# Fewer, larger first loads and four side-by-side first groups in a fused SiLU feed-forward kernel

## The chip, the cores and the metric

The kernel runs on one core of a Trainium2 chip. The metric is device time in microseconds of one execution. Only executions in the fast state are compared, and in each job the kernel before ran on the same chip as the others.

## The reference

The reference is a two-layer feed-forward block with SiLU, and its gradients. All inputs are bfloat16: x and grad_out are 2048 x 640, w1 is 640 x 1536, w2 is 1536 x 640.

```python
h = x @ w1
out = silu(h) @ w2
# outputs: out, and the gradients of x, w1 and w2 for grad_out
```

That is six matrix products of the same size: h, out, and four in the backward pass.

## The kernel before

The kernel works on the 2048 rows in four chunks of 512. In the first chunk it does, on the tensor engine (PE): 26 warm-up matmuls on a constant; 20 transposes of x (four row tiles of 128, five column blocks of 128) through PSUM; then 12 "h groups" of five 128x512 matmuls each, one group per block of 128 hidden columns; then the 60 matmuls of the first w2 phase, and so on. Only the start matters: what is loaded first, in which pieces, and what the first h matmuls wait for.

```python
# loads, in order of issue; nc.sync and nc.scalar are two DMA queues
load_x_tile(nc.sync, 0)      # x_nat[:, st, :], 128 rows x 640, 160 KB
load_x_tile(nc.scalar, 1)
load_x_tile(nc.sync, 2)
load_x_tile(nc.scalar, 3)
for lo, hi in ((0, 2), (2, DT)):          # row blocks of 128; DT = 5; FH = 256
    nc.sync.dma_start(out=w1_nat[:, lo:hi, 0:FH], in_=w1_v[:, lo:hi, 0:FH])
load_w1(FH, FC)                           # columns 256 to 512, all rows
for fc in range(1, NFC):
    load_w1(fc * FC, (fc + 1) * FC)       # columns 512 to 1024, 1024 to 1536
...
for hf in range(2):                       # w2 in two column halves
    nc.sync.dma_start(out=w2_nat[:, :, hf * DH:(hf + 1) * DH], in_=w2_v[...])
...
def pe_x_tile(xT, st):                    # per row tile: 5 transposes, 2 copies out of PSUM
    for lo, hi, copy in ((0, DS, nc.vector.tensor_copy), (DS, DT, nc.scalar.copy)):
        tp = ps_h.tile([P, hi - lo, P], dt_in, name="tp", tag="hp")
        for dt_ in range(lo, hi):
            nc.tensor.transpose(tp[:, dt_ - lo, :], x_nat[:, st, dt_ * P:(dt_ + 1) * P], ident[:])
        copy(out=xT[:, lo:hi, st * P:(st + 1) * P], in_=tp[:])
...
def h_group(ft, xT, aT, ghT):
    hp = ps_h.tile([P, SC], FP32, name="hp")
    for dt_ in range(DT):                 # five row blocks of w1, one after another
        nc.tensor.matmul(hp[:], lhsT=w1_nat[:, dt_, ft * P:(ft + 1) * P], rhs=xT[:, dt_, :],
                         start=(dt_ == 0), stop=(dt_ == DT - 1))
    # ... Silu and Tanh on ScalarE, two VectorE operations
...
for ft in range(FT):                      # FT = 12, first chunk
    h_group(ft, xT, aT, ghT)
```

Of the kernel before, what the change touches and what calls it, by code (L numbers as in the profile page):

```python
# [10 lines left out]
FP32 = mybir.dt.float32  # L11
# [4 lines left out]
def kernel(  # L16
# [11 lines left out]
    nc = tc.nc  # L28
    P = 128
# [6 lines left out]
    S, D = x2.shape  # L36
    F = w1.shape[1]
    ST, DT, FT = S // P, D // P, F // P
    SC = 512
    NCH = S // SC  # L40
    STC = SC // P
    DH = D // 2
    FC = 512
    NFC = F // FC
    LAG = 2
    NWARM = 26
    NFILL = 4
    dt_in = x.dtype
# [4 lines left out]
    ps_h = ctx.enter_context(tc.tile_pool(name="ps_h", bufs=8, space=bass.MemoryType.PSUM))  # L53
# [8 lines left out]
    x_nat = natpool.tile([P, ST, D], dt_in, name="x_nat")  # L62

    w1_v = w1.rearrange("(dt p) f -> p dt f", p=P)
    w2_v = w2.rearrange("(ft p) d -> p ft d", p=P)
    x_v = x2.rearrange("(st p) d -> p st d", p=P)
# [17 lines left out]
    with ExitStack() as mctx:  # L84
# [7 lines left out]
        warm = nc.const_aps.tensor(1.0, (P, P), dt_in)  # L92
        warm_a = cpool.tile([P, 1], FP32, name="warm_a")
        wp = ps_h.tile([P, SC], FP32, name="wp", tag="hp")
        for i in range(NWARM):
            nc.tensor.matmul(wp[:, 0:P], lhsT=warm, rhs=warm, start=True, stop=True)

        ident = cpool.tile([P, P], dt_in, name="ident")
        make_identity(nc, ident[:])

        w1_nat = w1pool.tile([P, DT, F], dt_in, name="w1_nat", tag="w1a")
        w2T = wpool.tile([P, DT, F], dt_in, name="w2T")
        w2_nat = wpool.tile([P, FT, D], dt_in, name="w2_nat")
# [9 lines left out]
            nc.sync.dma_start_transpose(out=goT[:], in_=go2[c * SC:(c + 1) * SC, :])  # L113
            return goT

        FH = FC // 2
        xT_next = xpool.tile([P, DT, SC], dt_in, name="xT")

        def load_w1(lo, hi):
            nc.sync.dma_start(out=w1_nat[:, :, lo:hi], in_=w1_v[:, :, lo:hi])  # L120

        def load_x_tile(eng, st):
            eng.dma_start(out=x_nat[:, st, :], in_=x_v[:, st, :])  # L123

        load_x_tile(nc.sync, 0)
        load_x_tile(nc.scalar, 1)
        load_x_tile(nc.sync, 2)
        load_x_tile(nc.scalar, 3)
        for lo, hi in ((0, 2), (2, DT)):
            nc.sync.dma_start(out=w1_nat[:, lo:hi, 0:FH], in_=w1_v[:, lo:hi, 0:FH])  # L130
        load_w1(FH, FC)
        for fc in range(1, NFC):
            load_w1(fc * FC, (fc + 1) * FC)
        nc.scalar.activation(warm_a[:], warm[:, 0:1], ACT.Silu)
        for hf in range(2):
            nc.sync.dma_start(out=w2_nat[:, :, hf * DH:(hf + 1) * DH], in_=w2_v[:, :, hf * DH:(hf + 1) * DH])
        goT_next = load_goT(0)
        for fc in range(NFC):
            nc.sync.dma_start_transpose(out=w2T[:, :, fc * FC:(fc + 1) * FC], in_=w2[fc * FC:(fc + 1) * FC, :])
        nc.sync.dma_start_transpose(out=w1T[:], in_=w1[:, :])  # L140

        DS = 3

        def pe_x_tile(xT, st):
            for lo, hi, copy in ((0, DS, nc.vector.tensor_copy), (DS, DT, nc.scalar.copy)):
                tp = ps_h.tile([P, hi - lo, P], dt_in, name="tp", tag="hp")
                for dt_ in range(lo, hi):
                    nc.tensor.transpose(tp[:, dt_ - lo, :], x_nat[:, st, dt_ * P:(dt_ + 1) * P], ident[:])  # L148
                copy(out=xT[:, lo:hi, st * P:(st + 1) * P], in_=tp[:])  # L149

        for st in range(STC):
            pe_x_tile(xT_next, st)
        for i in range(NFILL):
            nc.tensor.matmul(
                wp[:, 0:P], lhsT=ident[:], rhs=x_nat[:, STC - 1, 0:P], start=True, stop=True
            )

        def h_group(ft, xT, aT, ghT):
            hp = ps_h.tile([P, SC], FP32, name="hp")
            for dt_ in range(DT):  # L160
                nc.tensor.matmul(  # L161
                    hp[:],
                    lhsT=w1_nat[:, dt_, ft * P:(ft + 1) * P],
                    rhs=xT[:, dt_, :],
                    start=(dt_ == 0),
                    stop=(dt_ == DT - 1),
                )
            nc.scalar.activation(aT[:, ft, :], hp[:], ACT.Silu)  # L168
            t = tpool.tile([P, SC], FP32, name="t")
            nc.scalar.activation(t[:], hp[:], ACT.Tanh, scale=0.5)  # L170
            v = tpool.tile([P, SC], dt_in, name="v")
            nc.vector.tensor_scalar(out=v[:], in0=t[:], scalar1=-0.5, scalar2=0.5, op0=ALU.mult, op1=ALU.add)  # L172
            nc.vector.scalar_tensor_tensor(  # L173
                out=ghT[:, ft, :], in0=aT[:, ft, :], scalar=1.0, in1=v[:], op0=ALU.subtract, op1=ALU.mult
            )

        def g_group(ft, goT, ghT):
            gp = ps_h.tile([P, SC], FP32, name="hp")
# [32 lines left out]
        for c in range(NCH):  # L211
            xT, goT = xT_next, goT_next
            aT = apool.tile([P, FT, SC], dt_in, name="aT")
            ghT = apool.tile([P, FT, SC], dt_in, name="ghT")

            if c + 1 < NCH:
                xT_next = load_xT(c + 1)
                goT_next = load_goT(c + 1)
            if c == 1:
                for j in range(0, ST, STC):  # L220
                    nc.sync.dma_start(out=go_nat[:, j:j + STC, :], in_=go_v[:, j:j + STC, :])
            if c == 2:
                for j in range(STC, ST, STC):
                    nc.sync.dma_start(out=x_nat[:, j:j + STC, :], in_=x_v[:, j:j + STC, :])

            if c == 0:
                for ft in range(FT):
                    h_group(ft, xT, aT, ghT)
                nc.sync.dma_start(
                    out=aT_scr[:, c * SC:(c + 1) * SC].rearrange("(ft p) s -> p ft s", p=P), in_=aT[:]  # L230
                )
                sd_phase(c, w2_nat, aT, oT_scr)
                for ft in range(FT):
                    g_group(ft, goT, ghT)
                nc.sync.dma_start(
                    out=ghT_scr[:, c * SC:(c + 1) * SC].rearrange("(ft p) s -> p ft s", p=P), in_=ghT[:]
                )
                sd_phase(c, w1T, ghT, gxT_scr)
                continue

            for i in range(FT + LAG):
                if i < FT:
                    h_group(i, xT, aT, ghT)
                if i >= LAG:
                    g_group(i - LAG, goT, ghT)

            store_rows(c - 1, opool)
            nc.sync.dma_start(
                out=aT_scr[:, c * SC:(c + 1) * SC].rearrange("(ft p) s -> p ft s", p=P), in_=aT[:]
            )  # L250
            nc.sync.dma_start(
                out=ghT_scr[:, c * SC:(c + 1) * SC].rearrange("(ft p) s -> p ft s", p=P), in_=ghT[:]
            )
            if c == NCH - 1:
                load_a_blk(0, w1pool, "w1a")

            sd_phase(c, w2_nat, aT, oT_scr)
            sd_phase(c, w1T, ghT, gxT_scr)

    with ExitStack() as fctx:  # L260
        ab2pool = fctx.enter_context(tc.tile_pool(name="ab2pool", bufs=NFC - 1))
        gbpool = fctx.enter_context(tc.tile_pool(name="gbpool", bufs=NFC))
        fpool = fctx.enter_context(tc.tile_pool(name="fpool", bufs=NFC))
        s1pool = fctx.enter_context(tc.tile_pool(name="s1pool", bufs=3))

        for fc in range(1, NFC):
            load_a_blk(fc, ab2pool)
# [7 lines left out]

        gw2_v = gw2.rearrange("(ft p) d -> p ft d", p=P)
        g2T_v = g2T_scr[:].rearrange("(dt p) f -> p dt f", p=P)
        FB = FC // P
        k = 0
        for fc in range(NFC):  # L280
            a_blk = a_blks[fc]
            g2T = fpool.tile([P, DT, FC], dt_in, name="g2T")
            for dt_ in range(DT):
                gp = ps_h.tile([P, FC], FP32, name="hp")
                for st in range(ST):
                    nc.tensor.matmul(  # L286
                        gp[:],
                        lhsT=go_nat[:, st, dt_ * P:(dt_ + 1) * P],
                        rhs=a_blk[:, st, :],
                        start=(st == 0),  # L290
                        stop=(st == ST - 1),
# [8 lines left out]
        def store_gw2(fc):  # L300
            g2 = fpool.tile([P, FB, D], dt_in, name="g2")
            nc.sync.dma_start_transpose(out=g2[:], in_=g2T_scr[:, fc * FC:(fc + 1) * FC])
            nc.sync.dma_start(out=gw2_v[:, fc * FB:(fc + 1) * FB, :], in_=g2[:])

        gw1_v = gw1.rearrange("(dt p) f -> p dt f", p=P)
        k = 0
        for fc in range(NFC):
            gh_blk = gh_blks[fc]
            for dt_ in range(DT):
                if dt_ == DT // 2:  # L310
                    store_gw2(fc)
                if fc == NFC - 1 and dt_ == DT - 1:
                    for k, (lo, hi) in enumerate(((0, FC - P), (FC - P, FC))):
                        gp = ps_h.tile([P, FC], FP32, name="hp")
                        for st in range(ST):
                            nc.tensor.matmul(  # L316
                                gp[:, lo:hi],
                                lhsT=x_nat[:, st, dt_ * P:(dt_ + 1) * P],
                                rhs=gh_blk[:, st, lo:hi],
                                start=(st == 0),  # L320
                                stop=(st == ST - 1),
# [4 lines left out]
                        else:  # L326
                            nc.vector.tensor_copy(out=g1[:, lo:hi], in_=gp[:, lo:hi])  # L327
                        nc.sync.dma_start(
                            out=gw1_v[:, dt_, fc * FC + lo:fc * FC + hi], in_=g1[:, lo:hi]
# [3 lines left out]
                for st in range(ST):  # L333
                    nc.tensor.matmul(  # L334
                        gp[:],
                        lhsT=x_nat[:, st, dt_ * P:(dt_ + 1) * P],
                        rhs=gh_blk[:, st, :],
                        start=(st == 0),
                        stop=(st == ST - 1),
# [38 lines left out]
```

## Time and profile before

The time before is 322.19 us, median of three runs (321.62 to 322.34). In the profile PE is the tensor engine, PEld its loads of weights, DVE VectorE, ACT ScalarE, and SPq and ACTq the queues that issue loads. These lines are from the page of the kernel before: the span, the busy time of the engines, the chain that ended last by engine and by line, and the group of the h matmuls (busy us, mean ns of one, idle time before it and what ended most of it). Line 161 is the h matmul, line 196 a later phase.

```profile
span 320.5 us, 3556 instructions
...
PE 314.0 (98%) x1477; PEld 145.9 (46%) x1506; DVE 101.8 (32%) x179; ACT 78.6 (25%) x142; POOL 0.7 (0%) x6
...
PE 97%; DMA 1%; issue 1%; ACT 0%; SPq 0%; DVE 0%; DVEq 0%
PE hp L196 32%; PE hp L180 16%; PE hp L286 16%; PE hp L161 16%; PE hp L334 15%; DMA x_nat<-in_x_dram 1%; PE hp L316 1%; ACT xT L149 0%; PE tp L148 0%; SPq L123 0%; DVE g_2366 L327 0%; DVEq L327 0%
...
L161 PE MATMUL hp<-xT,w_nat 128*128 128x512 bf16 x232 | 56.4, 379 | 0.6 <-ACT xT L149 0.2
...
```

PE is busy 98% of the span and is 97% of the chain. The next lines are the timeline of PE in the first 9 us: start, duration, engine, line, operation, count, and in brackets the idle time before and its releaser. Line 148 is the transposes, 154 four filler matmuls, 161 the h matmuls.

```profile
...
start us, us, engine line op out<-in xcount [idle before <-releaser]
...
3.62 0.74 PE L148 MATMUL tp<-ident,x_nat 128*128 128x128 bf16 x10
5.32 0.73 PE L148 MATMUL tp<-ident,x_nat 128*128 128x128 bf16 x10 [0.96 <-DMA x_nat<-in_x_dram]
5.88 0.39 PE L154 MATMUL wp<-x_nat,ident 128*128 128x128 bf16 x4
6.48 2.75 PE L161 MATMUL hp<-xT,w_nat 128*128 128x512 bf16 x11 [0.21 <-ACT xT L149]
```

The first ten transposes (tiles 0 and 1) run at 3.62 us, the second ten only at 5.32, after a wait for x. The first h matmul starts at 6.48. From there 60 h matmuls take until 19.43, where the next phase begins: 12.95 us, or 60 times 215.8 ns, with nothing lost.

```profile
...
19.43 2.75 PE L196 MATMUL hp<-aT,w_nat 128*128 128x512 bf16 x12
...
```

The chain, in order of time (start, duration, what), names the same wait:

```profile
...
1.19 4.09 DMA x_nat<-in_x_dram
6.91 10.74 PE hp L161 x49
...
```

The DMA view, restricted to the first 5 us, gives for each group of loads its queue, count, size and the median time from issue to landing:

```profile
...
x_nat<-in_x_dram ACTq DMA_DIRECT2D x2, 160.0 KB, 3.7
x_nat<-in_x_dram SPq DMA_DIRECT2D x2, 160.0 KB, 3.5
...
w_nat<-in_w_dram SPq DMA_DIRECT2D x1, 192.0 KB, 4.3
w_nat<-in_w_dram SPq DMA_DIRECT2D x1, 128.0 KB, 4.1
```

A load is spread over 16 partial completions, and a wait ends with the last of them (the third x tile was complete at 5.27 us, and its transposes began at 5.32). The trace's completion records show how far the last is from the middle one (us from the span's start):

```
kernel before            8th of 16   16th of 16
x tile 0, 1              3.22, 3.39  3.57, 3.74
x tile 2, 3              4.01, 4.33  5.27, 5.50
w1 rows 0-256, 128 KB    4.73        5.78
w1 rows 256-640, 192 KB  5.43        6.43
w1 columns 256-512       6.51        7.39
```

### The profile page before, as it was taken

The page shows a single profiled execution, that of the slowest core. Times are in us where ns is not written, and L with a number is a line of the kernel's source. Part 1 is how long each engine was busy: PE and PEld are TensorE (multiplying, and loading weights), DVE is VectorE, ACT ScalarE, POOL GpSimd, SP SyncE. Part 2 cuts the span into 40 slices and gives each one's busy share as a digit, 9 for nine tenths or more (in the row PEclk, how much of TensorE's full clock was granted, in tenths as well). Part 3 has the DMA queues.
Part 4 walks back from the last instruction along what each step waited for, and adds up shares of the span by engine and source line. Part 5 has one row for each costly group of instructions (what it writes and reads, how often), then busy time and mean ns, then how long its engine had stood idle before and what let it go on. Part 6 is the DMA issues. An engine that isn't in the chain of part 4 may idle for free.

```text
span 320.5 us, 3556 instructions
## 1 busy us (share of the span) xinstructions
PE 314.0 (98%) x1477; PEld 145.9 (46%) x1506; DVE 101.8 (32%) x179; ACT 78.6 (25%) x142; POOL 0.7 (0%) x6
## 2 busy tenths in 40 slices
PE   7999999999999999999999999999999999999996
PEld 5444444444444444444444444444444444444443
DVE  1871551477510087810147741000000100001001
ACT  3960001555201255411054520110100001001100
POOL 0000000000000000000000000000000000000000
PEclk9999999999999999999999999999999999999999
DMA  8999999999699884392445079819999999995011
GB/s 246 316 192 209 254 265 253 320 271 277 215 229 336 203 237 122 118 319 66 127 159 141 2 254 268 217 25 293 262 240 263 249 203 343 251 281 181 33 49 35
DMA packets 149264, 66.69 MB, mean 208 GB/s; under 512 B 112640, under 2 KB 149248, under 8 KB 149248
## 3 DMA queue, kind: packets, MB, share of 16 engines
q1 hardware_dynamic: 148960, 66.13, 80.8%
q10 hardware_dynamic: 288, 0.33, 0.3%
q8 instruction: 12, 0.20, 0.2%
q14 instruction: 4, 0.03, 0.0%
HBM read 9.18 MB, written 28.97 MB: 119 GB/s over the span
## 4 chain that ended last, share of the span: by engine, by line
PE 97%; DMA 1%; issue 1%; ACT 0%; SPq 0%; DVE 0%; DVEq 0%
PE hp L196 32%; PE hp L180 16%; PE hp L286 16%; PE hp L161 16%; PE hp L334 15%; DMA x_nat<-in_x_dram 1%; PE hp L316 1%; ACT xT L149 0%; PE tp L148 0%; SPq L123 0%; DVE g_2366 L327 0%; DVEq L327 0%
## 5 line engine op out<-in xcount | busy, mean ns | idle before, releaser
L161 PE MATMUL hp<-xT,w_nat 128*128 128x512 bf16 x232 | 56.4, 379 | 0.6 <-ACT xT L149 0.2
L180 PE MATMUL hp<-goT,w2T 128*128 128x512 bf16 x238 | 56.8, 379 | 0.1
L196 PE MATMUL hp<-aT,w_nat 128*128 128x512 bf16 x235 | 52.2, 379 | 0.3
L196 PE MATMUL hp<-ghT,w1T 128*128 128x512 bf16 x235 | 52.2, 379 | 0.3
L286 PE MATMUL hp<-a_blk,go_nat 128*128 128x512 bf16 x236 | 51.8, 379 | 0.2
L334 PE MATMUL hp<-gh_blk,x_nat 128*128 128x512 bf16 x219 | 48.2, 379 | 0.3
L204 ACT ACTIVATE oT<-hp 128x512 bf16<-128x512 f32 x24 | 14.3, 597 | 110.0 <-PE hp L196 110.0
L168 ACT ACTIVATE aT<-hp 128x512 bf16<-128x512 f32 x48 | 28.7, 597 | 31.7 <-PE hp L161 31.7
L196 PEld LDWEIGHTS <-w_nat 128*128 128x128 bf16 x240 | 23.5, 98 | 28.3
L180 PEld LDWEIGHTS <-w2T 128*128 128x128 bf16 x240 | 23.5, 98 | 28.3
L286 PEld LDWEIGHTS <-go_nat 128*128 128x128 bf16 x240 | 23.5, 98 | 28.3
L161 PEld LDWEIGHTS <-w_nat 128*128 128x128 bf16 x240 | 23.4, 98 | 28.4 <-issue 0.4
L196 PEld LDWEIGHTS <-w1T 128*128 128x128 bf16 x240 | 23.4, 98 | 28.4
L206 DVE CAST oT<-hp 128x512 bf16<-128x512 f32 x16 | 11.1, 692 | 78.0 <-PE hp L196 78.0
L187 DVE SCALAR_TENSOR_TENSOR ghT<-ghT,hp 128x512 bf16<-128x512 bf16 x48 | 32.5, 682 | 7.3 <-PE hp L180 7.3
L334 PEld LDWEIGHTS <-x_nat 128*128 128x128 bf16 x224 | 21.9, 98 | 26.4
L173 DVE SCALAR_TENSOR_TENSOR ghT<-aT,v 128x512 bf16<-128x512 bf16 x48 | 33.0, 688 | 0.6
L172 DVE TENSOR_SCALAR v<-t 128x512 bf16<-128x512 f32 x48 | 20.5, 427 | 29.2 <-ACT t L170 29.2
L170 ACT ACTIVATE t<-hp 128x512 f32<-128x512 f32 x48 | 28.4, 591 | 0.0
L296 DVE CAST g2T<-hp 128x512 bf16<-128x512 f32 x7 | 4.8, 692 | 46.1 <-PE hp L286 46.1
L294 ACT ACTIVATE g2T<-hp 128x512 bf16<-128x512 f32 x8 | 4.8, 598 | 47.0 <-PE hp L286 40.7
L343 ACT ACTIVATE g_2140<-hp 128x512 bf16<-128x512 f32 x1 | 0.6, 597 | 13.6 <-DMA out_dram<-g_2077 13.6
(33 smaller groups left out, 29.3 us busy)
## 6 DMA issues: line engine op xcount, KB each, us to landing
aT_scr<-aT SPq DMA_DIRECT2D x4, 1536.0 KB, 6.7
ghT_scr<-ghT SPq DMA_DIRECT2D x4, 1536.0 KB, 8.0
out_dram<-o_sb SPq DMA_DIRECT2D x8, 640.0 KB, 3.4
oT_scr<-oT SPq DMA_DIRECT2D x4, 640.0 KB, 3.9
go_nat<-in_grad_out_dram SPq DMA_DIRECT2D x4, 640.0 KB, 8.1
gxT_scr<-oT SPq DMA_DIRECT2D x4, 640.0 KB, 4.7
w_nat<-in_w_dram SPq DMA_DIRECT2D x2, 960.0 KB, 10.9
x_nat<-in_x_dram SPq DMA_DIRECT2D x3, 640.0 KB, 7.8
```

The source lines that it names most:

```text
L161: nc.tensor.matmul(hp[:], lhsT=w1_nat[:, dt_, ft * P:(ft + 1) * P], rhs=xT[:, dt_, :], start=(dt_ == 0), stop=(dt_ == DT - 1),)
L168: nc.scalar.activation(aT[:, ft, :], hp[:], ACT.Silu)
L170: nc.scalar.activation(t[:], hp[:], ACT.Tanh, scale=0.5)
L172: nc.vector.tensor_scalar(out=v[:], in0=t[:], scalar1=-0.5, scalar2=0.5, op0=ALU.mult, op1=ALU.add)
L173: nc.vector.scalar_tensor_tensor(out=ghT[:, ft, :], in0=aT[:, ft, :], scalar=1.0, in1=v[:], op0=ALU.subtract, op1=ALU.mult)
L180: nc.tensor.matmul(gp[:], lhsT=w2T[:, dt_, ft * P:(ft + 1) * P], rhs=goT[:, dt_, :], start=(dt_ == 0), stop=(dt_ == DT - 1),)
L187: nc.vector.scalar_tensor_tensor(out=ghT[:, ft, :], in0=ghT[:, ft, :], scalar=1.0, in1=gp[:], op0=ALU.add, op1=ALU.mult)
L196: nc.tensor.matmul(op_[:], lhsT=w_all[:, ft, dt_ * P:(dt_ + 1) * P], rhs=rhs_all[:, ft, :], start=(ft == 0), stop=(ft == FT - 1),)
L204: nc.scalar.activation(oT[:, dt_, :], op_[:], ACT.Copy)
L206: nc.vector.tensor_copy(out=oT[:, dt_, :], in_=op_[:])
L286: nc.tensor.matmul(gp[:], lhsT=go_nat[:, st, dt_ * P:(dt_ + 1) * P], rhs=a_blk[:, st, :], start=(st == 0), stop=(st == ST - 1),)
L334: nc.tensor.matmul(gp[:], lhsT=x_nat[:, st, dt_ * P:(dt_ + 1) * P], rhs=gh_blk[:, st, :], start=(st == 0), stop=(st == ST - 1),)
```

## The change

The intent is to start h earlier and not to stall after that. x comes in three loads (1, 1 and 2 tiles) instead of four. The first 512 columns of w1 come as two row pieces (256 rows, 256 KB; 384 rows, 384 KB) instead of three pieces of half width. x is transposed by pairs of tiles, one copy per column block. And the first four h groups run side by side over w1's first 256 rows: eight matmuls need the first piece only, and while they run the second can land. As a side effect each DMA packet of the early w1 pieces is 1024 bytes instead of 512. w2 comes in one load, and the Tanh half of the SiLU work lags by four groups. The four filler matmuls now read the constant and not x.

```diff
-        load_x_tile(nc.sync, 0)
-        load_x_tile(nc.scalar, 1)
-        load_x_tile(nc.sync, 2)
-        load_x_tile(nc.scalar, 3)
-        for lo, hi in ((0, 2), (2, DT)):
-            nc.sync.dma_start(out=w1_nat[:, lo:hi, 0:FH], in_=w1_v[:, lo:hi, 0:FH])
-        load_w1(FH, FC)
+        load_x_tiles(nc.sync, 0, 1)
+        load_x_tiles(nc.scalar, 1, 2)
+        load_x_tiles(nc.sync, 2, STC)
+        load_w1_rows(nc.sync, 0, KM)      # w1_nat[:, lo:hi, 0:FC]; KM = 2
+        load_w1_rows(nc.sync, KM, DT)
...
-        for hf in range(2):
-            nc.sync.dma_start(out=w2_nat[:, :, hf * DH:(hf + 1) * DH], in_=w2_v[...])
+        nc.sync.dma_start(out=w2_nat[:], in_=w2_v[:])
...
+        def pe_x_pair(xT, st):
+            for dt_ in range(DT):
+                tp = ps_h.tile([P, 2, P], dt_in, name="tp", tag="hp")
+                for q in range(2):
+                    nc.tensor.transpose(tp[:, q, :], x_nat[:, st + q, dt_ * P:(dt_ + 1) * P], ident[:])
+                copy = nc.scalar.copy if dt_ % 2 else nc.vector.tensor_copy
+                copy(out=xT[:, dt_, st * P:(st + 2) * P], in_=tp[:])
...
+        def h_first(xT, aT, ghT):
+            hps = []
+            for ft in range(FB):                       # FB = 4
+                hps.append(ps_h.tile([P, SC], FP32, name="hp"))
+            for dt_ in range(KM):
+                for ft in range(FB):
+                    h_mm(hps[ft], ft, xT, dt_, dt_ + 1)
+            for i in range(FT + LAG_G):                # LAG_G = 4
+                if i < FT:
+                    if i < FB:
+                        h_mm(hps[i], i, xT, KM, DT)
+                    else:
+                        hps.append(ps_h.tile([P, SC], FP32, name="hp"))
+                        h_mm(hps[i], i, xT, 0, DT)
+                    silu_a(i, hps[i], aT)
+                if i >= LAG_G:
+                    silu_grad(i - LAG_G, hps[i - LAG_G], aT, ghT)
...
-                for ft in range(FT):
-                    h_group(ft, xT, aT, ghT)
+                h_first(xT, aT, ghT)
```

More of the change, by code (lines that the diff above doesn't have):

```diff
@@ L41 @@
     STC = SC // P
-    DH = D // 2
     FC = 512
     NFC = F // FC
+    FB = FC // P
     LAG = 2
+    LAG_G = 4
+    KM = 2
     NWARM = 26
@@ L114, in load_goT @@
             return goT
-        FH = FC // 2
         xT_next = xpool.tile([P, DT, SC], dt_in, name="xT")
@@ L120, in load_w1, with load_x_tiles, load_w1_rows @@
             nc.sync.dma_start(out=w1_nat[:, :, lo:hi], in_=w1_v[:, :, lo:hi])
-        def load_x_tile(eng, st):
-            eng.dma_start(out=x_nat[:, st, :], in_=x_v[:, st, :])
-        load_x_tile(nc.sync, 0)
-        load_x_tile(nc.scalar, 1)
-        load_x_tile(nc.sync, 2)
-        load_x_tile(nc.scalar, 3)
-        for lo, hi in ((0, 2), (2, DT)):
-            nc.sync.dma_start(out=w1_nat[:, lo:hi, 0:FH], in_=w1_v[:, lo:hi, 0:FH])
-        load_w1(FH, FC)
+        def load_x_tiles(eng, lo, hi):
+            eng.dma_start(out=x_nat[:, lo:hi, :], in_=x_v[:, lo:hi, :])
+        def load_w1_rows(eng, lo, hi):
+            eng.dma_start(out=w1_nat[:, lo:hi, 0:FC], in_=w1_v[:, lo:hi, 0:FC])
+        load_x_tiles(nc.sync, 0, 1)
[3 more added lines that the diff above has]
+        load_w1_rows(nc.sync, KM, DT)
         for fc in range(1, NFC):
@@ L134 @@
         nc.scalar.activation(warm_a[:], warm[:, 0:1], ACT.Silu)
-        for hf in range(2):
-            nc.sync.dma_start(out=w2_nat[:, :, hf * DH:(hf + 1) * DH], in_=w2_v[:, :, hf * DH:(hf + 1) * DH])
+        nc.sync.dma_start(out=w2_nat[:], in_=w2_v[:])
         goT_next = load_goT(0)
@@ L140, with h_mm @@
         nc.sync.dma_start_transpose(out=w1T[:], in_=w1[:, :])
-        DS = 3
-        def pe_x_tile(xT, st):
-            for lo, hi, copy in ((0, DS, nc.vector.tensor_copy), (DS, DT, nc.scalar.copy)):
-                tp = ps_h.tile([P, hi - lo, P], dt_in, name="tp", tag="hp")
-                for dt_ in range(lo, hi):
-                    nc.tensor.transpose(tp[:, dt_ - lo, :], x_nat[:, st, dt_ * P:(dt_ + 1) * P], ident[:])
-                copy(out=xT[:, lo:hi, st * P:(st + 1) * P], in_=tp[:])
-        for st in range(STC):
-            pe_x_tile(xT_next, st)
-        for i in range(NFILL):
-            nc.tensor.matmul(
-                wp[:, 0:P], lhsT=ident[:], rhs=x_nat[:, STC - 1, 0:P], start=True, stop=True
-            )
-        def h_group(ft, xT, aT, ghT):
-            hp = ps_h.tile([P, SC], FP32, name="hp")
-            for dt_ in range(DT):
+        def pe_x_pair(xT, st):
[5 more added lines that the diff above has]
+                copy(out=xT[:, dt_, st * P:(st + 2) * P], in_=tp[:])
+        pe_x_pair(xT_next, 0)
+        for i in range(NFILL):
+            nc.tensor.matmul(wp[:, 0:P], lhsT=warm, rhs=warm, start=True, stop=True)
+        pe_x_pair(xT_next, 2)
+        def h_mm(hp, ft, xT, lo, hi):
+            for dt_ in range(lo, hi):
                 nc.tensor.matmul(
@@ L167, in h_group, with silu_a, silu_grad @@
                 )
+        def silu_a(ft, hp, aT):
             nc.scalar.activation(aT[:, ft, :], hp[:], ACT.Silu)
+        def silu_grad(ft, hp, aT, ghT):
             t = tpool.tile([P, SC], FP32, name="t")
@@ L175, in h_group @@
             )
+        def h_group(ft, xT, aT, ghT):
+            hp = ps_h.tile([P, SC], FP32, name="hp")
+            h_mm(hp, ft, xT, 0, DT)
+            silu_a(ft, hp, aT)
+            silu_grad(ft, hp, aT, ghT)
+        def h_first(xT, aT, ghT):
[15 more added lines that the diff above has]
+                    silu_grad(i - LAG_G, hps[i - LAG_G], aT, ghT)
         def g_group(ft, goT, ghT):
@@ L277 @@
         g2T_v = g2T_scr[:].rearrange("(dt p) f -> p dt f", p=P)
-        FB = FC // P
         k = 0
```

## The prediction

> **What bounds the kernel now.** The tensor engine: busy 98% of the 320.5 us span on the page, 97% of the chain of waits. The main work is 1440 matmuls of 128x512, 215.8 ns apart in the timeline. The Trainium skill, "TensorE: Matmul & The Clock Gate", section "Back-to-back issue gap", gives N/2.4+2.5 ns, 216 for 512, as the warm gap: the trace agrees. So 1440 x 0.2158 = 310.8 us is fixed. The first such matmul starts at 6.48 us; the last output follows the last matmul by 3 us. The 60 matmuls of the first h phase take 6.48 to 19.43, exactly 60 gaps: no stall after the start. The change can only move the start, unless it makes a new stall.
>
> **What sets 6.48.** The four x tiles (160 KB each, two per queue) land at 3.57, 3.74, 5.27 and 5.50 us (DMA landings). Most of a tile's 16 partial completions come about 1 us earlier (tile 3: eighth at 4.33, last at 5.50): one DMA engine lags, with three packets of about 400 ns instead of 55. The Trainium skill, "DMA: Bandwidth & Descriptors", section "Why a DMA increments its semaphore by 16 and not by 1", says only the full count means all landed; the trace shows the wait ending on the last. Then: transposes to 6.05, last DVE copy to 6.33, matmul at 6.48, 0.98 us after the last landing. The w1 pieces land at 5.78, 6.43 and 7.39, only just off the path.
>
> **What the change does.**
> - x: the same 640 KB, but on SP's queue tiles 2 and 3 go wholly before w1. In the kernel before, w1 had moved perhaps a third of its first 8 KB per engine before tile 3 was in, some 0.13 us. Last x landing about 5.35.
> - Transposes by pair: the first h matmul needs only the first column block (two transposes, one 128x256 copy, estimated 0.29 us from 358 ns for 384 columns). Landing to matmul about 0.8 us instead of 0.98.
> - w1's first piece grows from 128 to 256 KB. 1024-byte packets take 47 to 51 ns (27 for 512 bytes), so 16 per engine is about 0.8 us: landing about 6.1, a tie with the copy.
> - First h matmul about 6.15, gain 0.3 us.
> - The eight side-by-side matmuls buy 8 x 0.216 = 1.7 us, to about 7.9, before w1's second piece (about 7.2) is needed. No stall.
> - The lag of 4 delays tanh and DVE work by about 2.7 us; PSUM's eight buffers cover it. The backward groups need ghT 13 us later. Nothing on the path.
> - w2 in one load must be whole by about 19.1; both halves were in at 17.76 before, and larger packets are no slower.
>
> **Time.** 322.19 - 0.35 = 321.8 us; 8 in 10: 321.0 to 322.4. Faster by over 2%: 0.005; within 2%: 0.99; slower: 0.005.
>
> **What would show it.** First 128x512 matmul of h at 6.0 to 6.3 us, and 12.95 us from it to the next phase's first; its releaser w1's first piece or the second pair's first copy; last x landing 5.2 to 5.4; no PE idle at the ninth h matmul; everything after shifted by one constant.
>
> **What would make it wrong.** The lagging DMA engine may be an accident of a run: without it the start comes up to 1 us earlier (about 5.4); with a worse one the change shows nothing. A stall at the ninth matmul (second w1 piece late), at the first w2 matmul, or on PSUM would cost. The range of before's three runs, 0.7 us, is as large as the gain.

## The result and the profile after

The changed kernel took 322.19 us (median of four runs, 321.70 to 322.71), the kernel before 322.21 us (four runs, 321.62 to 322.34). The ratio of the fast runs is 1.0003 with a 95% interval of 0.998 to 1.0027: the same. A ratio here is the record's own comparison of the fast runs; it is close to the ratio of their means, and not quite that of the medians quoted beside it. A second sample of five runs, below, gave 1.0013 (1.0000 to 1.0026). There is no gain to be seen, and in these few runs the times of the changed kernel are more spread: over 1.0 and 1.2 us in the two samples, against 0.7 and 0.6 us for the runs of before beside them.

The lines of the page of the changed kernel that answer to those above; line 158 is now the h matmul:

```profile
span 320.0 us, 3585 instructions
...
PE 315.9 (99%) x1506; PEld 146.1 (46%) x1506; DVE 101.5 (32%) x181; ACT 77.5 (24%) x142; POOL 0.7 (0%) x6
...
PE 97%; DMA 2%; SPq 0%; issue 0%; DVE 0%; DVEq 0%
...
L158 PE MATMUL hp<-xT,w_nat 128*128 128x512 bf16 x240 | 57.0, 379 | 0.5 <-DVE xT L149 0.4
...
```

The profiled run was one of the changed kernel's faster ones (321.79 us). The timeline of PE from 3.5 us; line 147 is the transposes:

```profile
...
3.93 1.58 PE L147 MATMUL tp<-ident,x_nat 128*128 128x128 bf16 x20
5.88 1.90 PE L158 MATMUL hp<-xT,w_nat 128*128 128x512 bf16 x8 [0.37 <-DVE xT L149]
7.93 1.25 PE L158 MATMUL hp<-xT,w_nat 128*128 128x512 bf16 x5
```

h starts at 5.88 us, 0.60 us earlier than in the kernel before. But eight matmuls later the tensor engine has to wait: the ninth starts at 7.93. The weight loads (PEld) say for what:

```profile
...
5.88 1.41 PEld L158 LDWEIGHTS <-w_nat 128*128 128x128 bf16 x8 [0.54 <-DMA w_nat<-in_w_dram]
7.93 0.33 PEld L158 LDWEIGHTS <-w_nat 128*128 128x128 bf16 x3 [0.64 <-DMA w_nat<-in_w_dram]
```

Both starts wait for w1: the first piece, complete at 5.84, and the second, complete at 7.89. The line of PE above names a copy (`DVE xT`) for the first start instead, and the last copy on DVE did end at 5.84 too. But the first h matmul needs only column block 0 of both pairs, and by the instruction records the copy of that block, the fourth on DVE, ended at 5.40; in three_again h started at 6.06, before the last two DVE copies had ended (6.17 and 6.56). So w1's first piece cost about 0.44 us even in this trace. The copies:

```profile
...
4.31 1.53 DVE L149 COPY xT<-tp 128x256 bf16<-128x256 bf16 x6 [4.31 <-PE tp L147]
...
```

The chain has changed its first link from x to w1's second piece, issued at 2.16 us. It counts the phase after h (L221) from the end of the last h matmul, 19.33; the first matmul of that phase starts at 19.17:

```profile
...
2.16 5.72 DMA w_nat<-in_w_dram
7.93 11.40 PE hp L158 x52
19.33 12.95 PE hp L221 x60
...
```

```profile
...
19.17 3.19 PE L221 MATMUL hp<-aT,w_nat 128*128 128x512 bf16 x14
...
```

The loads of the first 5 us in the DMA view:

```profile
...
w_nat<-in_w_dram SPq DMA_DIRECT2D x1, 384.0 KB, 5.7
x_nat<-in_x_dram SPq DMA_DIRECT2D x1, 320.0 KB, 3.5
w_nat<-in_w_dram SPq DMA_DIRECT2D x1, 256.0 KB, 4.2
x_nat<-in_x_dram ACTq DMA_DIRECT2D x1, 160.0 KB, 3.2
x_nat<-in_x_dram SPq DMA_DIRECT2D x1, 160.0 KB, 3.0
...
```

The second piece took 5.7 us from issue to landing, at 7.89. The h phase is 13.28 us long instead of 12.95, so 0.33 of the 0.60 us are given back, and the next phase begins at 19.17 instead of 19.43, about 0.26 us earlier. From there to the last matmul it is 297.83 us in both traces (and in every fast trace), so nothing later in the kernel changes: the Tanh lag and the single w2 load cost nothing.

That makes one number useful for the rest: the **effective start**, the start of the phase after h minus 12.95 us, which is when h would have to start to reach that point without a stall. It is 6.48 us in the trace of before and 6.22 in this trace of after. A run's time minus its effective start is 315.6 to 315.9 us in all thirteen fast traces, so the time of a run is, to about 0.15 us, its effective start plus a constant.

### The profile page after: what moved, and what is told of

The parts are those of the page before. It is cut to its first block, busy times and chain, and to the rows that moved or that the text cites. A ratio compares the mean times of both kernels' runs of the same rounds, so it can differ in the third digit from the quotient of the medians.

```text
span 320.0 us, 3585 instructions
## 1 busy us (share of the span) xinstructions
PE 315.9 (99%) x1506; PEld 146.1 (46%) x1506; DVE 101.5 (32%) x181; ACT 77.5 (24%) x142; POOL 0.7 (0%) x6
## 4 chain that ended last, share of the span: by engine, by line
PE 97%; DMA 2%; SPq 0%; issue 0%; DVE 0%; DVEq 0%
PE hp L221 32%; PE hp L205 16%; PE hp L309 16%; PE hp L158 16%; PE hp L357 15%; DMA w_nat<-in_w_dram 2%; PE hp L339 1%; SPq L124 0%; SPq L127 0%; DVE g L350 0%; DVEq L350 0%
## 5 line engine op out<-in xcount | busy, mean ns | idle before, releaser
L221 PE MATMUL hp<-aT,w_nat 128*128 128x512 bf16 x240 | 52.5, 379 | 0.0
L221 PE MATMUL hp<-ghT,w1T 128*128 128x512 bf16 x240 | 52.5, 379 | 0.0
L167 ACT ACTIVATE aT<-hp 128x512 bf16<-128x512 f32 x48 | 30.0, 627 | 33.3 <-PE hp L158 33.3
L221 PEld LDWEIGHTS <-w_nat 128*128 128x128 bf16 x240 | 23.5, 98 | 28.3
L221 PEld LDWEIGHTS <-w1T 128*128 128x128 bf16 x240 | 23.4, 98 | 28.4
L171 ACT ACTIVATE t<-hp 128x512 f32<-128x512 f32 x48 | 29.9, 628 | 0.0
L368 DVE CAST g<-hp 128x512 bf16<-128x512 f32 x7 | 4.8, 692 | 47.0 <-PE hp L357 26.3
```

Of the source, the lines that this page charges most:

```text
L167: nc.scalar.activation(aT[:, ft, :], hp[:], ACT.Silu)
L171: nc.scalar.activation(t[:], hp[:], ACT.Tanh, scale=0.5)
L221: nc.tensor.matmul(op_[:], lhsT=w_all[:, ft, dt_ * P:(dt_ + 1) * P], rhs=rhs_all[:, ft, :], start=(ft == 0), stop=(ft == FT - 1),)
```

## The experiments

Twelve more runs were made; with the first two that is fourteen traces of ten kernels. This table has one row per fast trace, in us from the span's start, from the trace's completion and instruction records. The first w1 piece is given with its size and its 8th and 16th completion; "full clock" is where the granted clock of PE (the share of full speed that it is allowed) is first recorded as full (the first three-piece trace has no such record; there the transposes go from 107 ns apart to 56 ns at about 4.5 us).

```
trace            x last  first w1 piece        second  full clock  h first  h long  eff. start  run
before           5.50    128 KB  4.73 / 5.78   6.43    3.67        6.48     12.95   6.48        322.23
before_again     4.75    128 KB  4.93 / 5.11   6.18    6.57        6.35     13.04   6.44        322.20
x_only_again     4.57    128 KB  4.70 / 5.17   6.07    3.49        5.78     12.95   5.77        321.50
after            4.74    256 KB  5.20 / 5.84   7.89    4.06        5.88     13.28   6.22        321.79
after_again      4.54    256 KB  5.09 / 6.71   8.68    4.66        6.75     13.20   7.01        322.67
no_second_piece  4.60    256 KB  5.28 / 6.73   7.82    6.55        6.78     12.96   6.79        322.44
w2_halves        4.69    256 KB  5.06 / 6.96   8.01    4.33        7.00     12.96   7.02        322.78
in_order         4.63    256 KB  5.17 / 6.08   7.46    3.44        6.12     13.92   7.09        322.80
w1_first         5.74    256 KB  4.07 / 4.32   8.11    3.65        6.45     12.95   6.45        322.02
packets_512      4.85    128 KB  4.71 / 5.24   5.66    6.35        6.06     13.50   6.61        322.35
three_pieces     4.46    128 KB  4.80 / 5.88   6.55    -           5.92     12.96   5.94        321.57
three_again      4.72    128 KB  4.67 / 5.86   6.63    6.07        6.06     12.96   6.07        321.85
five_pieces      4.66    128 KB  4.77 / 5.57   5.97    6.72        6.06     13.61   6.72        322.58
```

Two things must be kept in mind when these rows are compared. The clock: in five traces it is late (6.07 to 6.72), and the transposes are then 107 ns apart instead of 56; with the changed loads they keep PE busy until 6.06, which is where h starts in three_again, packets_512 and five_pieces, so a first piece that lands before that cannot show there. The chip: before_again and experiments 2 to 4 ran on chip 13; x_only, packets_512, three_pieces and w1_first on 6; the other four on 12 (the chip of the first comparison is not on record). The three latest first pieces (6.71, 6.73, 6.96) are all of chip 13. On chip 12 alone, 256 KB landed at 6.08, 128 KB of the same packets at 5.86 and 5.57, and 128 KB of 512-byte packets at 5.17: the order is the same, the differences are smaller. How much of the late landing belongs to the chip was not tested.

### 1. The kernel before, again

No edit. The question was whether the slow x tiles of the first trace belong to the kernel.

> The kernel before, unchanged, for a second trace of its start. If one lagging DMA engine belongs to the kernel, the last x landing is again 5.3 to 5.6 us, about 1 us after the eighth of its sixteen completions, and h starts at 6.4 to 6.6 us. If the lag is an accident of the run, the last x landing moves by several tenths of a microsecond, and h's start with it. Time ratio to before 1.000 within 0.002.

Measured: 322.20 us (321.73 to 322.39), ratio 1.0002 (0.9989 to 1.0015). The last x tile landed at 4.75 us, not 5.50. So the late x on which my reading of the start rested does not belong to the kernel in every run. h nevertheless started at 6.35. The timeline of PE says why:

```profile
...
3.71 2.32 PE L148 MATMUL tp<-ident,x_nat 128*128 128x128 bf16 x20
...
6.35 2.84 PE L161 MATMUL hp<-xT,w_nat 128*128 128x512 bf16 x12
```

The 20 transposes took 2.32 us; in a trace where the clock was up early, ten of them take 0.73 (experiment 8). In this trace the full clock is recorded only from 6.57 us, so the transposes were slow and the first h matmuls too. Two different causes gave nearly the same effective start, 6.48 and 6.44. That is chance.

The Trainium skill, "TensorE: Matmul & The Clock Gate", section "What's actually happening", describes a clock gate that opens after a busy window of about 3.4 us, and says that the window is free-running and the opening therefore differs from run to run. The traces agree that it differs, but not in size: the page puts the variation at 500 ns either way, and here, with the same 26 warm-up matmuls from 0.78 us on, the full clock is recorded from 3.44 to 6.72 us. In four traces it is there by 3.67, less than 3 us after the first matmul, so a whole busy window was not needed. I had cited this page and left this part out of the prediction.

### 2. The changed kernel, again

No edit.

> The changed kernel, unchanged, for a second trace. Theory A (the late second w1 piece belongs to the change): h starts at about 5.9 us, the second piece lands again at 7.5 us or later, and the ninth h matmul waits 0.2 us or more. Rival B (the slow packets were an accident of that run): the second piece lands near 7.2 us or earlier and there is no wait. Time ratio to before 0.999 to 1.000.

Measured: 322.25 us (322.03 to 323.23), ratio 1.0013 (1.0000 to 1.0026). This is the weight-load timeline:

```profile
...
6.75 1.41 PEld L158 LDWEIGHTS <-w_nat 128*128 128x128 bf16 x8 [1.36 <-DMA w_nat<-in_w_dram]
8.72 0.33 PEld L158 LDWEIGHTS <-w_nat 128*128 128x128 bf16 x3 [0.56 <-DMA w_nat<-in_w_dram]
```

Theory A holds for the second piece, and a worse part, which I had not expected, comes on top: the first piece landed at 6.71, so h started at 6.75, 0.87 us later than in the other trace of the same kernel, although the eighth of its sixteen completions was in at 5.09. Then the ninth matmul waited again for the second piece, which landed at 8.68; this cost 0.25 us. The effective start is 7.01. The lag passes from load to load: the sixteenth completion trails the fifteenth by 0.84 us in the first piece, and by 1.19, 1.24 and 1.23 us in the three loads behind it.

### 3. Without the second piece (wrong result)

```diff
-                    lhsT=w1_nat[:, dt_, ft * P:(ft + 1) * P],
+                    lhsT=w1_nat[:, (dt_ % KM) if wrong else dt_, ft * P:(ft + 1) * P],
...
-                        h_mm(hps[i], i, xT, KM, DT)
+                        h_mm(hps[i], i, xT, KM, DT, wrong=True)
```

> Wrong h on purpose: the first four groups read w1's first piece again in place of the second, so nothing waits for the second. If the wait at the ninth matmul is what ate the rest of the gain, then h takes 12.95 us again from its first matmul to the next phase's first, which comes about 0.33 us earlier than in the changed kernel, 0.6 us earlier than before; time ratio to before about 0.998. If the wait was a symptom and the time is limited by something later (third w1 piece, ACT, PSUM), a wait of the same size appears later in the h phase.

Measured: 322.23 us (321.63 to 322.48), ratio 1.0002 (0.9988 to 1.0015); the output is wrong, as meant. h took 12.96 us: the wait is gone and no other appeared later, as the theory said. But the gain did not come: the expected ratio was about 0.998, the interval begins at 0.9988. In its trace the first piece landed at 6.73 and held h until 6.78. PE in this trace:

```profile
...
6.78 1.47 PE L158 MATMUL hp<-xT,w_nat 128*128 128x512 bf16 x6 [0.51 <-DMA w_nat<-in_w_dram]
```

So removing the second piece's wait is not enough for the gain; in this trace the first piece holds h. The wait may still have a price: beside the 1.0013 of the changed kernel in the same job, 1.0002 is about 0.3 us less, as much as the wait cost in the traces (0.33 and 0.25), but the intervals overlap.

### 4. w2 in two halves again

```diff
-        nc.sync.dma_start(out=w2_nat[:], in_=w2_v[:])
+        for hf in range(2):
+            nc.sync.dma_start(out=w2_nat[:, :, hf * DH:(hf + 1) * DH], in_=w2_v[:, :, hf * DH:(hf + 1) * DH])
```

> The changed kernel with w2 loaded in two halves as before. Rival C: the queue's free slot made the transposing load of grad_out be issued at 4.7 us instead of 9.9, and its preparation slowed the packets of w1's second piece. Then, with the issue late again, the second piece lands near 7.2 us and the ninth matmul does not wait. If C is wrong the second piece lands within the spread of the other traces of the changed kernel (about 7.9) and the wait stays.

Measured: 322.78 us (321.80 to 323.01), ratio 1.0016 (1.0003 to 1.0029), so a little slower than before. The first piece landed at 6.96 and the second at 8.01. With the later issue of grad_out's load restored, the pieces are as late as ever: rival C falls. There was no wait at the ninth matmul here only because h itself began at 7.00.

### 5. and 8. Only the x loads changed

```diff
-        load_x_tile(nc.sync, 2)
-        load_x_tile(nc.scalar, 3)
+        nc.sync.dma_start(out=x_nat[:, 2:STC, :], in_=x_v[:, 2:STC, :])
```

> The kernel before with only the x loads changed (tiles 2 and 3 in one load on SP's queue). Effective start is the first matmul of the phase after h minus 12.95 us; it was 6.47 and 6.44 in two traces of before and 6.22, 7.01 and 7.02 in three of the changed loads. Theory D (the larger w1 pieces with 1024-byte packets are what comes late): here w1's pieces stay as before, so the first lands at 5.1 to 5.9 and does not hold h; x lands at about 4.6, and effective start is 5.7 to 6.4, the lower end where the PE clock is up before the transposes. Time ratio to before 0.998 to 1.000. Rival E (moving x ahead only moves the slow packets onto w1): the first w1 piece lands at 6.2 or later here too, no gain.

Measured: 322.12 us as the median of the four fast runs (321.73 to 322.34), ratio 1.0005 (0.9992 to 1.0019). The fifth execution took 481.20 us, and it was the profiled one. Its span and granted clock:

```profile
...
core 0: 479.3 us, clock 0.658
...
```

That trace is not used for times. Its loads landed as elsewhere, x at 4.58 us and the first w1 piece at 4.96. The kernel ran again:

> The kernel before with only the x loads changed, again, because its profiled run fell in a state with a clock of 0.658. x lands at about 4.6, w1's first 128 KB piece in 512-byte packets at 5.0 to 5.8, and effective start is 5.7 to 6.6; which of the two decides depends on whether the PE clock is up before the transposes (start about 5.7) or after (about 6.3). Ratio to before 0.999 to 1.001: without the larger pieces there is neither the loss of the changed kernel nor a sure gain.

Measured: 322.01 us (321.50 to 322.23), ratio 0.9996 (0.9984 to 1.0008). In its trace the clock was up at 3.49 us:

```profile
...
3.55 0.73 PE L147 MATMUL tp<-ident,x_nat 128*128 128x128 bf16 x10
4.61 0.73 PE L147 MATMUL tp<-ident,x_nat 128*128 128x128 bf16 x10 [0.33 <-DMA x_nat<-in_x_dram]
...
5.77 3.40 PE L160 MATMUL hp<-xT,w_nat 128*128 128x512 bf16 x14 [0.21 <-ACT xT L148]
```

The last x landed at 4.57, the first w1 piece (128 KB) at 5.17, and h started at 5.78 without a stall. With the small pieces the first w1 piece does not hold h, as theory D expected; E, that x ahead makes w1 late, falls. But the mean time does not fall below that of before either (0.9996 and 1.0005, both intervals across 1): the one late x of the first trace is not what a typical run loses.

### 6. w1's row pieces as column halves

```diff
-        load_w1_rows(nc.sync, 0, KM)
-        load_w1_rows(nc.sync, KM, DT)
+        for lo, hi in ((0, KM), (KM, DT)):
+            for cl in (0, FC // 2):
+                nc.sync.dma_start(out=w1_nat[:, lo:hi, cl:cl + FC // 2], in_=w1_v[:, lo:hi, cl:cl + FC // 2])
```

> The changed kernel with each w1 row piece loaded as two column halves, so the packets are 512 bytes again and the volume before the first and the second piece is the same. If the slow packets come with the 1024-byte form, there are few here (under 12 over 150 ns between 3.5 and 6.5 us, against 18 to 27 in the changed kernel) and both halves of the first piece land by 5.9. If they come with the volume or the hour, the first piece lands at 6.2 to 7.0 again, and effective start stays near 7.0.

Measured: 322.35 us (321.68 to 322.49), ratio 1.0008 (0.9996 to 1.0021). The first 256 rows were in at 5.66 us (halves at 5.24 and 5.66), the rest at 7.00, and 11 packets between 3.5 and 6.5 us took over 150 ns (26 and 27 in the two traces of the changed kernel, 6 and 11 in those of before). So the expectation for the smaller form is met. Two things changed at once, though: packets of 512 bytes, and loads of half the size. And the time was not gained: the next load, columns 512 to 1024, was in only at 10.87, and the h phase was 13.50 us long (about 0.39 us of the excess is this wait, 0.15 the late clock).

### 7. w1's first columns in three pieces

```diff
-    KM = 2
+    KM = 3
...
-        load_w1_rows(nc.sync, 0, KM)
-        load_w1_rows(nc.sync, KM, DT)
+        for lo, hi in ((0, 1), (1, 3), (3, DT)):
+            load_w1_rows(nc.sync, lo, hi)
```

> The changed kernel with w1's first 512 columns in three pieces of 128, 256 and 256 rows, and the first three row blocks side by side. If volume per piece sets when h starts, the first piece (128 KB) lands at 5.0 to 5.9 and h starts at 5.4 to 6.0, and the second, needed 0.86 us later, or the third, needed 2.6 us later, decides: effective start 5.9 to 6.6, ratio 0.998 to 1.000. If one lagging engine holds the first piece whatever its size, it lands at 6.2 or later and nothing is gained.

Measured: 321.57 us (321.22 to 321.66), ratio 0.9987 (0.9973 to 1.0001). The weight loads:

```profile
...
5.92 3.14 PEld L158 LDWEIGHTS <-w_nat 128*128 128x128 bf16 x16 [0.59 <-DMA w_nat<-in_w_dram]
```

The first piece, 128 KB in 1024-byte packets, landed at 5.88 us, about where the changed kernel's lands in its best trace, and after it nothing waited: the second (6.55) came 0.23 us before it was needed and the third (7.29) over a microsecond before. All 512 first columns were in at 7.29. The effective start, 5.94, is the earliest but one of the thirteen.

Because the interval touches 1, it ran again:

> The three-piece kernel, unchanged, for a second trace and five more times. If its gain over before (0.24 us of medians in the first job) is not chance, the ratio to before is again 0.998 to 0.9995 and the median is below that of before by 0.2 us or more; effective start 5.7 to 6.3.

Measured: 321.82 us (321.50 to 322.09), ratio 0.9991 (0.9979 to 1.0003), effective start 6.07, first piece at 5.86; here the clock was late, and the transposes, not w1, held h until 6.06. The median is 0.30 us below that of before in the same job (322.12), and it was 0.24 below in the first job (321.81). Each interval alone still touches 1; the two agree in sign and size. This is the one version for which the runs suggest a gain over before, of about 0.1%; it was not run in one job with the changed kernel. It also speaks on packet size: its packets are 1024 bytes, its first piece is only 128 KB, and still 15 and 19 packets took over 150 ns (21 in experiment 11). So a smaller load does not by itself remove the slow packets.

### 9. w1's piece ahead of x

```diff
+        load_w1_rows(nc.sync, 0, KM)
         load_x_tiles(nc.sync, 0, 1)
         load_x_tiles(nc.scalar, 1, 2)
         load_x_tiles(nc.sync, 2, STC)
-        load_w1_rows(nc.sync, 0, KM)
         load_w1_rows(nc.sync, KM, DT)
```

> The changed kernel with w1's first piece issued before x on the same queue. If the slow packets belong to the time from 4 to 6 us, w1's piece lands on time (about 3.8, all sixteen completions within 0.4 us) and the x packets or the second w1 piece moving at 4 to 6 us are slow. If they belong to w1's 1024-byte row pieces, they come early, at 2 to 4 us, in the first piece, and again with the second. h starts when x is in and copied, 5.6 to 6.5 us.

Measured: 322.25 us (322.02 to 322.49), ratio 1.0010 (0.9998 to 1.0023). Neither expectation came true as a whole. The same 256 KB piece, moving first, was in at 4.32 us, 0.25 us after its eighth completion; and the load of two x tiles that now moved from 4 to 6 us was not slow either (eighth completion 5.45, last 5.74). Only 6 packets between 3.5 and 6.5 us took over 150 ns. One of sixteen completions of the second piece then came at 8.11, where the others were in by 6.79. So the tail belongs neither to the piece as such nor to the time from 4 to 6 us as such, and 1024-byte packets do not bring it by themselves: 576 of them started between 3.5 and 6.5 us, and 4 took over 150 ns. This is one trace. The cause of the tail stays open. For the time, this order is no use: x is now what h waits for (h first at 6.45).

### 10. The changed loads, but the groups one after another

```diff
-            for dt_ in range(KM):
-                for ft in range(FB):
-                    h_mm(hps[ft], ft, xT, dt_, dt_ + 1)
...
-                        h_mm(hps[i], i, xT, KM, DT)
+                        h_mm(hps[i], i, xT, 0, DT)
```

> The changed kernel with its loads, but the first four groups one after another. If the side-by-side order is what keeps the late second w1 piece off most of the path, the third matmul now waits for that piece (7.8 to 8.7 us in four traces), effective start is 7.4 to 8.3 instead of 6.2 to 7.0, and the time ratio to before is 1.003 to 1.006. If the first piece alone set the time (as in the runs where it landed at 6.7 to 7.0), the loss against the changed kernel is below 0.3 us.

Measured: 323.31 us (322.32 to 324.89, six runs), ratio 1.0045 (1.0023 to 1.0066), slower than before clear of noise, though under 2%. PE in its trace:

```profile
...
6.12 0.60 PE L158 MATMUL hp<-xT,w_nat 128*128 128x512 bf16 x2 [0.71 <-DMA w_nat<-in_w_dram]
7.51 1.69 PE L158 MATMUL hp<-xT,w_nat 128*128 128x512 bf16 x6 [0.78 <-DMA w_nat<-in_w_dram]
```

Two matmuls run at 6.12, then the third waits for the second piece, until 7.51: 0.97 us lost, and the effective start is 7.09, below the 7.4 to 8.3 expected, because the pieces were early here (6.08 and 7.46). Side by side, a late second piece costs 0.33 us at most in the traces. So this half of the change works, and is worth about 1 us (ratios of 1.0003 and 1.0013 with it, 1.0045 without); it pays back much of what the larger pieces take.

### 11. w1's first columns in five pieces

```diff
-    KM = 2
+    KM = 4
...
-        load_w1_rows(nc.sync, 0, KM)
-        load_w1_rows(nc.sync, KM, DT)
+        for dt_ in range(DT):
+            load_w1_rows(nc.sync, dt_, dt_ + 1)
```

> As the three-piece kernel, but w1's first 512 columns in five pieces of 128 rows, four row blocks side by side. The first piece is the same size, so h starts at 5.5 to 6.1; the second is needed 0.86 us later and is half as large, so the waits behind the start shrink below 0.1 us. Effective start 5.6 to 6.2, ratio 0.998 to 0.9995, about the same as three pieces. If the issue of two more loads (0.5 us each on SP) delays the later ones, a wait appears at the seventeenth or twenty-first matmul.

Measured: 322.76 us (322.45 to 323.21), ratio 1.0022 (1.0010 to 1.0034), a loss where I had expected a gain like that of three pieces. The five pieces were in by 7.11, in time, and the first at 5.57. But the next load is late:

```profile
...
10.27 0.10 PEld L158 LDWEIGHTS <-w_nat 128*128 128x128 bf16 x1
11.02 0.55 PEld L158 LDWEIGHTS <-w_nat 128*128 128x128 bf16 x4 [0.65 <-DMA w_nat<-in_w_dram]
```

Columns 512 to 1024 landed at 10.98 us (9.10 and 9.72 with three pieces), so the first group that needs them stalls, by about 0.32 us. (The other half of the 0.66 us by which h is longer in this trace is the late clock: the first two h matmuls take 0.43 and 0.33 us instead of 0.22.) Part of the late landing is the later issue, 4.08 us against 3.18. The rest I can't name: from 6 to 7 us the DMA engines were busy 73% and moved 226 GB/s, against 107% and 362 GB/s with three pieces, with data queued in both (the view's share of the DMA engines can pass 100%). The kernel of experiment 6, with four w1 pieces, shows the same dip (231 GB/s). What makes the dip was not tested.

## Why the prediction was right or wrong

The time was predicted as 321.8 us with a range of 321.0 to 322.4 and measured as 322.19; "within 2%" was right. The range reached from 1.2 us below before's own time to 0.2 us above it, so it held without the gain. That PE bounds the kernel, that only the start can move and that nothing later would (the lag, PSUM, w2 in one load) were right: 297.83 us from the phase after h to the last matmul in every fast trace. The gain of 0.35 us was not there: it would be a ratio of 0.9989, which the first interval (0.998 to 1.0027) still allows and the second (1.0000 to 1.0026) does not. Point by point:

- **"Last x landing about 5.35."** Measured 4.54 to 4.74 with the changed loads. But it was 4.75 in the second trace of before too. I took the lag of one trace for a part of the baseline, while naming as a risk that it might be an accident of a run. The second trace bears the risk out, and experiments 5 and 8 show no gain from the x loads alone.
- **"Landing about 6.1, a tie with the copy"** for the first w1 piece. This is the step that failed, in size. With the piece behind x, it landed at 5.84, 6.08, 6.71, 6.73 and 6.96 in five traces, while its eighth completion came at 5.06 to 5.28 in all of them. I costed the packets alone (16 per engine at about 49 ns, 0.8 us on top of the last x); the tail of the larger piece, 0.6 to 1.9 us behind the eighth completion, is the term that was mis-sized. That 6.1 lies inside the measured range is luck, since two errors offset each other: x came 0.6 to 0.8 us earlier than predicted, and the piece 1.1 to 2.3 us after x instead of 0.8. With 128 KB pieces of 512-byte packets behind x the first piece landed at 4.96 to 5.78 and did not set h's start in any of the traces (in two of the four fast ones h could not start before about 6.06 and 6.35 for the late clock). The Trainium skill, "DMA: Bandwidth & Descriptors", section "Why a DMA increments its semaphore by 16 and not by 1", has the reason why the tail counts and the middle doesn't; the traces in which w1 releases h agree, as h started about 0.04 us after the sixteenth completion (6.71 to 6.75, 6.96 to 7.00).
- **"w1's second piece (about 7.2) ... No stall."** Wrong: 7.46 to 8.68 in the five traces, and the ninth matmul waited in both traces of the changed kernel. It cost 0.33 us of the 0.60 gained in one, and 0.25 us in the other.
- **"8 x 0.216 = 1.7 us" bought by the side-by-side order.** Right as a mechanism, and worth more than I gave it: without it the kernel is 0.45% slower than before.
- **"Landing to matmul about 0.8 us instead of 0.98."** The time itself was not seen, since in the changed kernel's traces w1, not the copy, releases h. But the copy that the first h matmul needs ended 0.66 us after the last x landing in the first trace (5.40 after 4.74), so this step was, if anything, too cautious.
- **What I left out:** the moment at which PE's clock goes up, 3.4 to 6.7 us. It makes the transposes take 2.3 us or about 1.6. Whether it is a source of the 0.7 us spread of before is not shown: the two traces of before, with the clock early and late, took 322.23 and 322.20 us.

So where the expected gain went: the baseline's late x was partly chance; the larger first piece came later by about as much as the rest could give; and the side-by-side order covered most of the late second piece. The sum is about zero. Shown: that w1's pieces release h in the changed kernel (waits in the traces), that removing the second's wait alone does not bring the gain (experiment 3), and what the order is worth (10). Suggested by the runs: that smaller first pieces help (7, twice). Open: why the completions of the larger pieces trail when they follow x and not when they lead (9); what packet size and load size each do (6 changes both; 7 and 11 keep the packets and shrink the load, and have 15 to 21 slow packets); how much of it is the chip; and why five pieces slow the loads behind them (11).

## What to carry to other kernels

The first matmul waits for the sixteenth completion of its load, so cost the first loads by their last completions in several traces, not by the median rate or one trace. These runs suggest making the first piece as small as the work that it starts, and letting work that needs only that piece run side by side until the next lands. But change the number of early loads with care, because the load behind them can become the wait. When a start differs by several tenths of a microsecond between runs of the same kernel, take a second trace of the baseline before explaining a difference of that size.

## What the Trainium skill lacked or had wrong

- "DMA: Bandwidth & Descriptors", section "Bandwidth", gives a rule that favours batching (at least 1 MiB for 75% of peak, measured on another issuing path). Apart from a row on two DMA engines that are usually slower, which it ties to another issuing path, the page has nothing on the tail of a load's sixteen completions at a kernel's start. Here a 256 KB load behind 640 KB of x had its eighth completion at 5.06 to 5.28 us and its sixteenth at 5.84 to 6.96, and the same 1.3 MB of x and w1 was all in at 7.46 to 8.68 with two w1 pieces behind x, against 7.00 to 7.47 with three or more in seven fast traces. For what was needed first, larger was later in these traces.
- The same page, section "Specifications", puts the size for line rate at 512 bytes and above. In these traces a packet of 512 bytes took 27 ns in the median and one of 1024 bytes 46 to 47, so per byte and by the medians 512 was still 15 to 17% slower than 1024.
- "TensorE: Matmul & The Clock Gate" describes half clock, full clock, 13/16 once three cores of a die are busy, and a clock seen stuck at a quarter for a while. One execution here, on a single core, ran at a mean granted clock of 0.658 for its whole 479 us span (481.20 us, against 321.73 to 322.34 for the other four of the same kernel). No page that I used has this state. The page's ±500 ns for the moment at which the clock goes up is too narrow for these traces, which range over 3.3 us (experiment 1).
